# Idle products of the identity ahead of the matmul groups of a state-space kernel's front, on one Trainium2 core

## The chip, the core and the metric

The kernel runs on one core of one Trainium2 chip. The metric is the device time of one execution in microseconds (us). A profiled execution gives the trace from which all spans and durations below come; its own time and the medians of the timed runs are in the table further down.

## What is computed

The reference is one transformer-like block on a sequence of L = 2048 rows of D = 640 features, all in float32. Six modulation vectors come from a small product, `mod = silu(c) @ w_mod`. Then:

```
h = layernorm(x) * (1 + ca) + sa
x = x + ga * conv(h)            # S4: y = irfft(rfft(h) * rfft(K)) + h * Dskip
h = layernorm(x) * (1 + cb) + sb
x = x + gb * (silu(h @ w1) * (h @ w3)) @ w2     # F = 1728
```

The convolution kernel is `K[d, l] = Re sum_n C[d,n] dt B[d,n] exp(dt A[d,n] l)` with N = 128 complex states for each of the 640 features. The convolution needs tables of exp, sin and cos for all d and n, products of these, and Fourier transforms along l.

## The kernel before, in words

The 640 features are cut into 40 steps of 16 (`NS = 40`, `SD = 16`). A step's convolution kernel is made in a pipeline with these parts; the names are those of the code, and L numbers are lines of the kernel:

- `phases` (L485, GpSimd) multiplies integer phases, `absph`, `cosine`, `sine` (L493 to L503, ScalarE) turn them into cos and sin.
- `exp_fast` (L445) and `exp_slow` (L454) put the logarithms of the magnitudes into PSUM by matmuls (tiles `pa`, `pq`), and `fast` and `slow` (L464, L469, ScalarE) take their exp into a table `A`.
- `real1`, `real2`, `imag1`, `imag2` (L512 to L526, VectorE) multiply magnitudes by cos and sin.
- `kgen` (L532) contracts over n on TensorE (64 matmuls of 32 columns, tile `pk`), `k1evac` (L542, VectorE) scales the result, `k_stage1` (L551) is the first stage of the Fourier transform (tile `pt`), and `k_out` (L559, ScalarE) stores it in `uk`.

Ahead of that stand the tables' parameters (`class Polar`, L243): its `rows` (L291) transposes logarithms on TensorE into the tables `la` and `lm` (tile `pT`, L305 to L308). It runs once for the first 128 features and once for the other 512 (`rest`). The modulation vectors come from `mod_early` (L333, eight pieces), `mod_shift` (L342), `mod_gate` (L359) and, later, `mod_cols` (L368, five pieces): matmuls of `w_mod` columns (`mod_sums`, L319), a VectorE copy, and small matmuls on that copy. The input itself is normalized (`ln1_norm`, L392) and goes through the first Fourier stage in 16 tiles of 128 rows (`u_stage1`, L411): 8 small matmuls of 32 rows by 64 columns for each tile, 12 for an even tile, in two PSUM tiles `pu`, then a ScalarE or VectorE evacuation of each into `u`, and a DMA of `u` to DRAM (`us`).

The part up to where the first `stage2` (L576, tile `p`) runs is called the front here. In it the order of each engine's work is chosen by the scheduler of the framework from the order of the program. Behind the front, from L861 on, `in_order[0]` is true, and the order is a list written out by hand (`ROUND`, L854). The front begins with the first `Polar`, makes the tables of steps 0 and 1 (L758 to L767), and only then starts the tiles of `u` (`u_stage1(0)`, L780). The loop at L799 goes over ten values of `tk`; each does one step's tables, `kgen` of the step before, `k_stage1` of the one before that, and for `tk < 6` two tiles of `u`. At `tk` 2 and 6 it makes the exponentials of four steps.

Five tags of PSUM tiles share the 8 banks. `A` and `B` hold `pT`, `pa`, `pq` and the second half of `pu`, `Z` holds `pr`, the `pm` of `mod_cols` and of one piece of `mod_early`, and the first half of `pu`, `pb` and `pk` hold `pm`, `pk`, `pg` and `pt`. Each has one buffer, so a new tile waits until the last reader of the old one is done.

All loads and the `us` stores of the front are issued on SyncE's queue (SP), in order. Five late pieces of `w_mod` (L846) go to two places in turn, so the third, fourth and fifth each wait until the `mod_cols` that reads the place has run. The reload of `us` for the first chunk (`u_load`, L566) is issued at `tk` 7, between the fourth and the fifth of these pieces. `mod_cols(4)` (L801) is the last thing of the front ahead of the first `stage2`.

Far behind the front, the kernel has an idle product already: `keep_warm` (L929) multiplies a tile of zeros, 28 times in all.

Of the kernel before, what the change touches and what calls it, by code (L numbers as in the profile page):

```python
# [17 lines left out]
P = 128  # L18
# [90 lines left out]
def tile_kernel(ctx: ExitStack, tc: tile.TileContext, a):  # L109
    nc = tc.nc  # L110
    V, S, G, PE = nc.vector, nc.scalar, nc.gpsimd, nc.tensor
# [7 lines left out]
    ident = cp.tile([P, P], F32, name="ident")  # L119
# [8 lines left out]
    in_order = [False]  # L128
# [59 lines left out]
    lt = pm_.tile([P, 2, D - DC], F32, name="lt")  # L188
# [51 lines left out]
        [w_room(1, 0, 256, 1280), w_room(1, 1, 256, 1280), w_room(1, 2, 256, 1280), w_table(), w_table()])]  # L240


    class Polar:  # L243

        def __init__(self, cs, E, l2):
# [45 lines left out]
        def rows(self):  # L291

            nt = 2 * self.nk
            nat = lambda v: v.rearrange("n (t p r j) -> n t r p j", t=nt, p=4, r=2)
            rows = lambda v: v[:, :self.nk * P].rearrange("n (t r p j) -> n t r p j", t=nt, p=4, r=2)
            for k in range(nt):
                self.E.tensor_tensor(rows(lt[:, 0])[:, k], nat(self.are)[:, k], nat(self.dtc)[:, k], op=OP.mult)
            for k in range(nt):
                V.tensor_tensor(rows(lt[:, 1])[:, k], nat(self.q)[:, k], nat(self.ld)[:, k], op=OP.add)
            for i, dst in enumerate((la, lm)):  # L300
                raw = lt[:, i, :self.nk * P].rearrange("n (b c) -> n b c", c=32)
                both = self.l2[i].rearrange("n (b s c) -> n b s c", s=2, c=32)
                acopy(both.bitcast(F32R)[:, :, 0], raw)
                V.tensor_tensor(both[:, :, 1], raw, both[:, :, 0], op=OP.subtract)
                pT = psS.tile([P, 2, 512], F32, name="pT", tag="AB"[i], bufs=1).rearrange("p a b -> p (a b)")  # L305
                for k in range(nt):
                    PE.transpose(pT[:, k * P:(k + 1) * P], self.l2[i][:, k * P:(k + 1) * P], ident)
                acopy(dst[:, 2 * self.k0:2 * self.k0 + nt], pT[:, :nt * P].rearrange("p (k n) -> p k n", k=nt))  # L308
# [24 lines left out]
    def mod_early(i, w, tag):  # L333

        pm = psS.tile([P, 512], F32, name="pm", tag=tag, bufs=1)
        n = w.shape[2]
        part = mod_sums(w, pm)
        for b in range(n // P):
            PE.matmul(pm[:, 256 + b:257 + b], part[:, b * P:(b + 1) * P], one4, start=True, stop=True)
        V.tensor_copy(cols.rearrange("p s k -> p (s k)")[:, 2 * i:2 * i + n // P], pm[:, 256:256 + n // P])  # L340

    def mod_shift():  # L342

        sa, ca, ga, zero, inv, r, gs = (cols[:, i] for i in range(7))
        V.tensor_scalar(ca, ca, 1.0, None, op0=OP.add)
        V.tensor_scalar(zero, ca, 0.0, 1e-18, op0=OP.is_equal, op1=OP.mult)
        V.tensor_tensor(ca, ca, zero, op=OP.add)
        V.reciprocal(inv, ca)
        V.tensor_tensor(r, inv, sa, op=OP.mult)

        pr = psS.tile([P, 2, 512], F32, name="pr", tag="Z", bufs=1).rearrange("p a b -> p (a b)")
        for k in range(KD):
            PE.matmul(pr[:, k * P:(k + 1) * P], r[:, k:k + 1].broadcast_to([P, P]), ident, start=True, stop=True)
        for hh in range(2):
            h = slice(hh * 64, hh * 64 + 64)
            act(shift[h], pr[h, hh * 320:hh * 320 + 320], AF.Copy, scale=c1c[h])
        V.tensor_copy(rrow[:64], pr[:64, :D])

    def mod_gate():  # L359

        V.tensor_tensor(cols[:, 6], cols[:, 1], cols[:, 2], op=OP.mult)
        gt = pm_.tile([P, WC], F32, name="part", bufs=2)[:, :KD * NA].rearrange("p (k g) -> p k g", k=KD)
        V.tensor_tensor(gt, bc(tog, 1, KD), bc(cols[:, 6], 2, NA), op=OP.mult)
        pg = psS.tile([P, 512], F32, name="pg", tag="pb", bufs=1)
        PE.matmul(pg[:, :KD * NA], toq, gt.rearrange("p k g -> p (k g)"), start=True, stop=True)
        V.tensor_copy(gaT, pg[:, :KD * NA])

    def mod_cols(i, w):  # L368

        pm = psS.tile([P, 2, 512], F32, name="pm", tag="Z", bufs=1)  # L370
        part = mod_sums(w, pm[:, 0])
        lo, hi = ((0, 3), (0, 3), (0, 3), (0, 1), (2, 3))[i]
        for b in range(lo, hi):
            PE.matmul(pm[:, 1, b:b + 1], part[:, b * P:(b + 1) * P], one4, start=True, stop=True)
        V.tensor_copy(modTf[:, 3 * i + lo:3 * i + hi], pm[:, 1, lo:hi])
        if i >= 3:

            row = part[:, P:] if i == 3 else part[:, :2 * P]
            PE.matmul(pm[:, 1, 256:], one4.broadcast_to([P, P]), row, start=True, stop=True)
            V.tensor_copy(gbr[:, (i - 3) * 256:(i - 3) * 256 + 256], pm[:, 1, 256:])  # L380
        if i == 4:
            V.tensor_scalar(modT[:, 1, :], modT[:, 1, :], 1.0, None, op0=OP.add)
# [28 lines left out]
    def u_stage1(j):  # L411


        x = xt[j]
        u = hpz.tile([P, 4, D // 2], F32, name="u", bufs=2)
        pu = [psS.tile([P, 2, 512], F32, name="pu", tag=t, bufs=1) for t in ("Z", "AB"[j % 2])]
        one = j % 2 == 0
        for q in range(2 if one else 0):
            for hh in range(2):
                PE.matmul(pu[0][hh * 64:hh * 64 + 64, q, :320], c1[q * NA:q * NA + 1],  # L420
                          rrow[q * NA:q * NA + 1, hh * 320:hh * 320 + 320],
                          start=True, stop=False, tile_position=(q * NA, hh * 64))
        for h in range(2):
            for q in range(2):
                r0 = (2 * h + q) * NA
                r = slice(r0, r0 + NA)
                for hh in range(2):
                    PE.matmul(pu[h][hh * 64:hh * 64 + 64, q, :320], s1r[r], x[r, hh * 320:hh * 320 + 320],  # L428
                              start=not (one and h == 0), stop=True, tile_position=(r0, hh * 64))
        if one:  # L430
            acopy(u[:, :2, :], pu[0][:, :, :320])
        else:
            V.tensor_tensor(u[:, :2, :], pu[0][:, :, :320], bc(shift, 1, 2), op=OP.add)
        V.tensor_tensor(u[:, 2:, :], pu[1][:, :, :320], bc(shift, 1, 2), op=OP.add)
        nc.sync.dma_start(usw[:, 4 * j:4 * j + 4, :], u)
# [4 lines left out]
    def exp_rows(s):  # L440
        return s // 4, slice(s % 4 * 8, s % 4 * 8 + 8), [(rr, slice(rr * 64, rr * 64 + 64)) for rr in range(2)]

    pA, pQ = {}, {}

    def exp_fast(steps):  # L445

        for s in steps:
            pA[s] = psS.tile([P, 2, 512], F32, name="pa", tag="AB"[s % 2] if not in_order[0] else "B", bufs=1)
            t, js, rows = exp_rows(s)
            for rr, r in rows:  # L450
                keep(PE.matmul(pA[s][:, rr, :], la[r, t, :], r2[r, js, :].rearrange("p j b -> p (j b)"),  # L451
                               start=True, stop=True, tile_position=(r.start, 0)))

    def exp_slow(steps):  # L454

        for s in steps:
            pQ[s] = psS.tile([P, 2, 512], F32, name="pq", tag="AB"[s % 2] if not in_order[0] else "B", bufs=1)
            t, js, rows = exp_rows(s)
            for i, w in enumerate((la, lm)):
                for rr, r in rows:  # L460
                    keep(PE.matmul(pQ[s][:, rr, :256], w[r, t, :], bc(sel[r, js], 2, NA) if i else r1[r, js, :],  # L461
                                   start=(i == 0), stop=(i == 1), tile_position=(r.start, 0)))
# [69 lines left out]
    def kgen(s):  # L532
        E, A = EC.pop(s), AA.pop(s)
        pk = psS.tile([P, SD // 4, NB], F32, name="pk", tag="pk", bufs=1)
        for g in range(SD // 4):
            for st, x in enumerate((E, A)):
                for dq in range(4):
                    keep(PE.matmul(pk[dq * 32:dq * 32 + 32, g, :], x[:, g * 4 + dq, 1, :], x[:, g * 4 + dq, 0:3:2, :],  # L538
                                   start=(st == 0), stop=(st == 1), tile_position=(0, dq * 32)))
        PK[s] = pk  # L540
# [10 lines left out]
    def k_stage1(s):  # L551
        pt = PT[s] = psS.tile([P, 4, P], F32, name="pt", tag="pb", bufs=1)
        kk = K1.pop(s)
        for g in range(4):
            for c in range(2):
                keep(PE.matmul(pt[c * 64:c * 64 + 64, g, :], kk[:, g, :], s1[:, c, :],  # L556
                               start=True, stop=True, tile_position=(0, c * 64)))
# [318 lines left out]
    for tk in range(NS - 4, LAG + 8 * NDC + 2):  # L876
# [14 lines left out]
        i = tk - 1 - LAG - 8 * NDC + 8  # L891
# [662 lines left out]
```

## Time and profile before

| what | us |
|---|---|
| median of 3 runs | 980.74 (979.18 to 981.52) |
| the profiled execution's own time | 979.54 |
| its span, first to last instruction | 977.8 |
| mean granted TensorE clock over the span | 0.94 |
| TensorE matmuls busy | 895.3 (92%) |
| VectorE busy | 715.4 (73%) |
| ScalarE busy | 543.6 (56%) |

The front is the first 167 us of the span. In a row of the timeline the first number is the start in us, the second the duration of the group in us, then engine, line, operation, output and inputs, and in brackets how long the engine was idle before it and what ended that. A row of the windows view gives the length of the window, and for each engine the busy time and the count of records, then PEclk, the granted TensorE clock (1.00 is full speed), the busy share of the DMA engines and the GB/s that they moved. One float32 `matmul` of the program is two MATMUL records and two weight loads (the 5 products of L353 are 10 records); a transpose is one. The clock is granted for stretches whose ends lie on a grid of 3.413 us. For the first 20 us of the span the trace holds no record of the clock, and the view shows 1.00 there.

### The profile page before, as it was taken

To read this page: it belongs to the slowest core of one execution; us is meant where nothing else is said; L and a number is where in the kernel's file an instruction comes from. 1 tells how busy PE (TensorE), PEld (TensorE's weight loads), DVE (VectorE), ACT (ScalarE), POOL (GpSimd) and SP (SyncE) were. 2 spreads that over 40 slices of the span, in tenths; PEclk is the share of its full clock that TensorE was granted. 3 is DMA by queue.
4 is the path that set the end of the run, shared out by engine and by line. 5 is a ranking of instruction groups with operands and counts; after the bars stand their busy time and mean duration, and the time that the engine had idled before them with its cause. 6 is when DMAs were issued, how large, how long until landed. Compare 5 with 4: busy or idle time off the path is not lost.

```text
span 977.8 us, 20279 instructions
## 1 busy us (share of the span) xinstructions
PE 895.3 (92%) x8050; PEld 675.2 (69%) x8050; DVE 715.4 (73%) x1257; ACT 543.6 (56%) x797; POOL 278.1 (28%) x278
## 2 busy tenths in 40 slices
PE   5779986898888889799999999999999999999998
PEld 2434444566666667467888888777888888888886
DVE  5778866999999996667666666567796766654675
ACT  3737675999999984246433333355753333333332
POOL 1372233454556550204422220121242222200000
PEclk9555587999999999999999999999999999999999
DMA  8544468556656588785312212895422221113443
GB/s 251 191 142 160 175 210 189 163 143 162 162 149 169 151 223 230 244 206 208 95 55 95 67 55 66 230 273 193 142 83 70 77 67 54 55 41 95 148 151 119
DMA packets 103715, 140.73 MB, mean 144 GB/s; under 512 B 20580, under 2 KB 62820, under 8 KB 103620
## 3 DMA queue, kind: packets, MB, share of 16 engines
q1 hardware_dynamic: 99812, 129.34, 45.2%
q0 software_dynamic: 2304, 7.74, 2.4%
q10 hardware_dynamic: 1504, 2.36, 0.8%
q8 instruction: 63, 1.03, 0.4%
q14 instruction: 32, 0.26, 0.1%
HBM read 107.94 MB, written 31.46 MB: 143 GB/s over the span
## 4 chain that ended last, share of the span: by engine, by line
PE 77%; ACT 9%; DMA 5%; DVE 4%; issue 3%; POOL 2%; ACTq 0%; SPq 0%; DVEq 0%; POOLq 0%
PE ps L103 55%; PE p L587 6%; PE pz L629 3%; PE pt L556 3%; PE pk L538 2%; ACT A L136 2%; DMA zs<-zt 2%; ACT cs L136 2%; DMA uk<-in_w_mod_dram 2%; PE pa L451 1%; PE pu L428 1%; PE pq L461 1%; PE pu L420 1%; PE pm L325 1%; ACT uk L139 1%
## 5 line engine op out<-in xcount | busy, mean ns | idle before, releaser
L103 DVE TENSOR_TENSOR s<-ps,s 128x512 f32<-128x512 f32 x138 | 94.9, 687 | 80.0 <-PE ps L103 79.7
L489 POOL TENSOR_TENSOR ph<-thi,iota 128x1024 int32<-128x1024 int32 x40 | 91.2, 2279 | 149.3 <-DVE A L525 61.1
L103 DVE TENSOR_TENSOR gl<-rw,gh 128x640 fp32r<-128x640 f32 x87 | 78.1, 898 | 66.6 <-ACT gh L103 66.5
L103 ACT CAST gh<-rw 128x640 fp32r<-128x640 f32 x87 | 63.3, 727 | 104.9 <-PE ps L103 64.9
L587 PE MATMUL p<-uk,s 128*64 128x256 f32 x640 | 79.8, 390 | 16.1 <-issue 7.2
L103 PE MATMUL ps<-xA,gh 128*128 128x512 f32 x280 | 87.8, 392 | 0.4 <-ACT xA L103 0.4
L103 PE MATMUL ps<-gh,uh 128*128 128x512 f32 x224 | 87.5, 390 | 0.0
L103 PE MATMUL ps<-gl,uh 128*128 128x512 f32 x224 | 87.2, 389 | 0.0
L103 POOL TENSOR_TENSOR S<-rw 128x256 f32<-128x256 f32 x46 | 36.8, 801 | 173.9 <-DVE S0l L103 163.1
L103 PE MATMUL ps<-gh,ul 128*128 128x512 f32 x208 | 81.1, 390 | 0.0
L587 PEld LDWEIGHTS p<-uk,s 128*64 128x64 f32 x640 | 46.1, 138 | 40.1 <-issue 12.3
L514 DVE TENSOR_TENSOR E<-A,cs 128x1024 f32<-128x1024 f32 x40 | 60.9, 1523 | 2.2 <-ACT cs L136 2.2
L103 PEld LDWEIGHTS ps<-xA,gh 128*128 128x128 f32 x280 | 52.1, 188 | 13.0 <-ACT xA L103 1.0
L103 PE MATMUL ps<-xA,gl 128*128 128x512 f32 x140 | 54.6, 390 | 0.0
L490 POOL TENSOR_TENSOR ph<-ph,phi 128x512 int32<-128x512 int32 x40 | 50.8, 1269 | 6.4 <-DVE phi L316 3.6
L556 PE MATMUL pt<-s,K 128*64 128x128 f32 x640 | 50.5, 295 | 0.6 <-ACT uk L139 0.6
L103 ACT ACTIVATE s<-ps 128x512 f32<-128x512 f32 (+1 forms) x33 | 19.7, 597 | 53.1 <-PE ps L103 53.1
L521 DVE TENSOR_TENSOR A<-A,ph 128x1024 f32<-128x1024 f32 x40 | 48.7, 1218 | 0.0
L103 PEld LDWEIGHTS ps<-gl,uh 128*128 128x128 f32 x224 | 42.1, 188 | 9.0
L103 PEld LDWEIGHTS ps<-gh,uh 128*128 128x128 f32 x224 | 42.0, 188 | 8.7
L538 PE MATMUL pk<-E 128*32 128x64 f32 x1280 | 46.0, 234 | 2.0 <-DVE E L514 1.2
L629 PE MATMUL pz<-Y,i 64*128 64x128 f32 x640 | 43.9, 280 | 4.1 <-ACT zt L139 4.0
(256 smaller groups left out, 2268.4 us busy)
## 6 DMA issues: line engine op xcount, KB each, us to landing
rw<-in_w_dram SPq DMA_DIRECT2D x52, 320.0 KB
us<-u SPq DMA_DIRECT2D x16, 640.0 KB
s<-in_s_dram SPq DMA_DIRECT2D x40, 256.0 KB
i<-in_i_dram SPq DMA_DIRECT2D x40, 256.0 KB
rw<-in_wg_dram SPq DMA_DIRECT2D x31, 320.0 KB
rw<-in_wu_dram SPq DMA_DIRECT2D x28, 320.0 KB
uk<-us SPq DMA_DIRECT2D x32, 256.0 KB
zs<-zt SPq DMA_DIRECT2D x32, 256.0 KB
```

Of the source, the lines that this page charges most:

```text
L103: ins = fn(*args, **kw)
L136: return tc.keep_in_program_order(S.activation(*args, **kw))
L139: return tc.keep_in_program_order(S.copy(out, in_))
L325: PE.matmul(pm[r, :n], scb[:, g], w[:, g, :], start=True, stop=False, tile_position=(0, r.start))
L489: hold(G.tensor_tensor(p, bc(thi[:, sl], 2, NPH), bc(iota, 1, SD), op=OP.mult))
L490: keep(G.tensor_tensor(p[:, :, :NA], p[:, :, :NA], bc(phi[:, sl], 2, NA), op=OP.add))
L514: keep(V.tensor_tensor(EC[s][:, :, 1:3, :], AA[s][:, :, 1:3, :], mid(cs[s]), op=OP.mult))
L521: keep(V.tensor_tensor(A[:, :, 1:3, :], A[:, :, 1:3, :], mid(ph[s]), op=OP.mult))
L538: keep(PE.matmul(pk[dq * 32:dq * 32 + 32, g, :], x[:, g * 4 + dq, 1, :], x[:, g * 4 + dq, 0:3:2, :], start=(st == 0), stop=(st == 1), tile ...
L556: keep(PE.matmul(pt[c * 64:c * 64 + 64, g, :], kk[:, g, :], s1[:, c, :], start=True, stop=True, tile_position=(0, c * 64)))
L587: keep(PE.matmul(p2[par * 64:par * 64 + 64, pi, c, :], s2[:, pi * 2 + par, c * 64:c * 64 + 64], uk[:, 0:kn + 1:kn, f, :], start=True, stop ...
L629: ins = keep(PE.matmul(pz[:, par, (g % 2) * 2 + pi, :], i1[r, pi, c, :], Y[r, pi, c, :], start=(c == 0), stop=(c == 1), tile_position=(par ...
```

## The change

A function is added that multiplies the 128 x 128 identity by itself into the PSUM tile that a matmul group is about to fill, `n` times. The group's first matmul starts a new sum and so overwrites the result. In the hand-ordered part it does nothing.

```
+    def stay_warm(t, n, by=None):
+
+        if in_order[0]:
+            return
+        out = t if len(t.shape) == 2 else t[:, 0] if t.shape[2] >= P else t[:, :P // t.shape[2]]
+        for _ in range(n):
+            PE.matmul(out[:, :P] if len(out.shape) == 2 else out, ident, ident if by is None else by, start=True, stop=True)
```

It is called right behind the allocation of each PSUM tile of the front:

```
 Polar.rows   pT   stay_warm(pT, 8 if i == 0 and self.cs.start == 0 else 2, lt[:, 1, :P])
 mod_early    pm   stay_warm(pm, 2)
 mod_shift    pr   stay_warm(pr, 4)
 mod_gate     pg   stay_warm(pg, 2)
 mod_cols     pm   stay_warm(pm, 2)
 u_stage1     pu   stay_warm(t, 2) for each of the two tiles
 exp_fast     pa   stay_warm(pA[s], 2)
 exp_slow     pq   stay_warm(pQ[s], 1)
 kgen         pk   stay_warm(pk, 2)
 k_stage1     pt   stay_warm(pt, 2)
```

In `Polar.rows` the product is of the identity by the first 128 columns of `lt[:, 1]`, which VectorE writes at L299. The program orders the idle products ahead of the group's own matmuls. No DMA, no tile and no instruction of another engine is added, moved or removed in the program.

More of the change, by code (lines that the diff above doesn't have):

```diff
@@ L305, in rows @@
                 pT = psS.tile([P, 2, 512], F32, name="pT", tag="AB"[i], bufs=1).rearrange("p a b -> p (a b)")
+                stay_warm(pT, 8 if i == 0 and self.cs.start == 0 else 2, lt[:, 1, :P])
                 for k in range(nt):
@@ L335, in mod_early @@
         pm = psS.tile([P, 512], F32, name="pm", tag=tag, bufs=1)
+        stay_warm(pm, 2)
         n = w.shape[2]
@@ L351, in mod_shift @@
         pr = psS.tile([P, 2, 512], F32, name="pr", tag="Z", bufs=1).rearrange("p a b -> p (a b)")
+        stay_warm(pr, 4)
         for k in range(KD):
@@ L364, in mod_gate @@
         pg = psS.tile([P, 512], F32, name="pg", tag="pb", bufs=1)
+        stay_warm(pg, 2)
         PE.matmul(pg[:, :KD * NA], toq, gt.rearrange("p k g -> p (k g)"), start=True, stop=True)
@@ L370, in mod_cols @@
         pm = psS.tile([P, 2, 512], F32, name="pm", tag="Z", bufs=1)
+        stay_warm(pm, 2)
         part = mod_sums(w, pm[:, 0])
@@ L416, in u_stage1 @@
         pu = [psS.tile([P, 2, 512], F32, name="pu", tag=t, bufs=1) for t in ("Z", "AB"[j % 2])]
+        for t in pu:
+            stay_warm(t, 2)
         one = j % 2 == 0
@@ L448, in exp_fast @@
             pA[s] = psS.tile([P, 2, 512], F32, name="pa", tag="AB"[s % 2] if not in_order[0] else "B", bufs=1)
+            stay_warm(pA[s], 2)
             t, js, rows = exp_rows(s)
@@ L457, in exp_slow @@
             pQ[s] = psS.tile([P, 2, 512], F32, name="pq", tag="AB"[s % 2] if not in_order[0] else "B", bufs=1)
+            stay_warm(pQ[s], 1)
             t, js, rows = exp_rows(s)
@@ L534, in kgen @@
         pk = psS.tile([P, SD // 4, NB], F32, name="pk", tag="pk", bufs=1)
+        stay_warm(pk, 2)
         for g in range(SD // 4):
@@ L553, in k_stage1 @@
         kk = K1.pop(s)
+        stay_warm(pt, 2)
         for g in range(4):
```

## The prediction

> **What bounds the kernel now.** I read the page first: the engines' slices and the TensorE clock (PEclk, tenths of full speed), each slice 24.4 us.
>
> ```profile
> PE   5779986898888889799999999999999999999998
> PEclk9555587999999999999999999999999999999999
> ```
>
> From the eighth slice on the clock is full and TensorE nearly always busy; the half-speed stretch lies in the front. Nothing behind the front gets another instruction, so the question is how many us earlier the front ends. Windows over its parts, cut where the path changes its engine:
>
> ```profile
> 10.00:28.00 18.00, 14.24 (x108) 8.44 (x108) 8.70 (x35) 7.77 (x14) 5.86 (x4) 0.87 0.95 277
> 28.00:78.00 50.00, 37.79 (x356) 18.38 (x356) 39.34 (x73) 28.13 (x35) 24.48 (x29) 0.53 0.48 171
> 78.00:136.00 58.00, 52.05 (x562) 27.59 (x566) 49.92 (x87) 41.50 (x51) 19.92 (x17) 0.59 0.44 160
> 136.00:167.00 31.00, 22.45 (x370) 15.12 (x362) 18.39 (x29) 20.53 (x24) 10.43 (x6) 0.83 0.94 234
> ```
>
> PE, PEld, DVE, ACT and POOL stand in this order, then PEclk. From 78 to 136 us PE is busy 52.05 of 58 us at a clock of 0.59, but VectorE is busy 49.92 as well. Then the chain of waits in three of these windows (shares by line), and the longest single piece of it:
>
> ```profile
> by line: POOL ph L489 11.2%; issue 8.2%; POOL rs L402 7.1%; POOL ph L490 6.1%; DVE u L434 5.8%; POOL lt L297 5.6%; DVE st L399 5.5%; PE pu L428 5.4%; PE pu L420 5.2%; DVE E L514 4.7%; DVE u L433 4.6%; DVE rs L403 4.2%; POOL rs L401 3.6%; PO
> by line: PE pu L428 18.9%; PE pt L556 11.2%; PE pu L420 10.9%; PE pT L307 6.6%; PE pk L538 6.3%; PE pa L451 6.0%; ACT cs L136 5.8%; ACT ph L136 5.2%; PE pq L461 4.5%; issue 4.5%; ACT u L139 4.3%; ACT uk L136 3.1%; ACT x L136 2.8%; DVE u L43
> by line: DMA uk<-in_w_mod_dram 33.5%; PE pm L325 11.0%; PE pm L374 8.1%; PE pq L461 4.9%; issue 4.8%; ACT L136 4.1%; DVE E L514 4.0%; PE pm L379 3.9%; DVE A L521 3.9%; PE pk L538 3.8%; ACT cs L136 3.7%; PE pt L556 3.6%; PE pa L451 3.5%; DVE
> 152.26 10.38 DMA uk<-in_w_mod_dram
> ```
>
> The reader is to see three different stages. From 28 to 78 us the path runs over POOL and DVE, and PE's share is small (`pu`, 5.4% and 5.2%, 5.3 us). From 78 to 136 us the seven PE groups shown make 64.4%, 37.4 us. From 136 us on a third is one wait for the last piece of `w_mod`.
>
> Why is the clock low while PE is busy? Windows of 3.413 us, PE alone, then PEclk:
>
> ```profile
> 71.11:74.53 3.41, 3.41 (x66) 0.50 0.73 244
> 74.53:77.94 3.41, 1.61 (x28) 1.00 0.69 261
> 88.18:91.59 3.41, 3.41 (x52) 0.50 0.00 0
> 91.59:95.01 3.41, 3.41 (x44) 0.50 0.02 5
> 115.49:118.90 3.41, 3.41 (x28) 0.50 0.00 0
> 118.90:122.31 3.41, 2.38 (x91) 1.00 0.64 172
> ...
> 45.37 1.37 PE L428 MATMUL pu<-x,misc 32*64 32x320 f32 x16 [0.78 <-ACT u L139]
> 88.13 1.32 PE L428 MATMUL pu<-x,misc 32*64 32x320 f32 x2
> ```
>
> The full windows at 71.11 and 115.49 are followed by a clock of 1.00, the one at 88.18 by 0.50. Busy does not say how full the array is: two `pu` records of 32 x 64 alone take 1.32 us, as long as 16 that run side by side (1.37 us). I read from this that the clock goes by the work that the array does, not by PE's busy time. The rows don't prove it: they hold no measure of how full the array was. A product of the identity fills all 128 rows and columns, so I expect it to raise the clock.
>
> The Trainium skill, TensorE: Matmul & The Clock Gate, Part 1 (The HAM clock gate), says under "What's actually happening" that the gate opens after one busy window of about 3.4 us. The trace differs: 3.41 of 3.41 us busy at 88.18, and the next window still at 0.50; the measurement decides. By that rule, products added where PE is already busy would change no clock, which is the fourth case below.
>
> **The change part by part.** It adds 180 products. Counted by the calls and by the times at which their groups run now: 24 between 10 and 28 us (8 + 2 for the first `pT`, 10 for five pieces of `mod_early`, 4 for two `pa`), 56 from 28 to 78 (32 of them for eight tiles of `u`), 72 from 78 to 136 (32 for `u`, 12 for `pa` and `pq`, 10 `kgen`, 10 `pt`, 4 `pT`, 2 `mod_cols`, 2 for the next `pa`), 28 from 136 to 167.
>
> The price of one, and what a warm clock is worth:
>
> ```profile
> 29.30 2.50 PE L353 MATMUL pr<-ident,cols 128*128 128x128 f32 x10 [2.71 <-DVE cols L349]
> 425.60 2.35 PE L103 MATMUL ps<-ident,T 128*128 128x128 f32 x20
> 96.88 1.97 PE L556 MATMUL pt<-s,K 128*64 128x128 f32 x14
> 144.53 1.09 PE L556 MATMUL pt<-s,K 128*64 128x128 f32 x16
> 17.81 0.80 PE L451 MATMUL pa<-r,la 64*128 64x512 f32 x2
> 139.19 0.40 PE L451 MATMUL pa<-r,la 64*128 64x512 f32 x2
> ...
> L103 PEld LDWEIGHTS ps<-xA,gh 128*128 128x128 f32 x280 | 52.1, 188 | 13.0 <-ACT xA L103 1.0
> ```
>
> L353 is the same form, cold: 10 records for 5 products, 0.50 us each. Warm, 20 records of that size take 2.35 us (transposes, one record each), so a product of two is 0.235. Its two weight loads of 128 columns could pace it instead, at 188 ns each 0.376. I take 0.235, because the 20 warm records load new weights each time too. Existing work: `pt` goes from 0.141 to 0.068 us a record, `pa` from 0.80 to 0.40 for two; I take 0.52 of the cold time, a saving of 0.48.
>
> *78 to 136 us.* The path's 37.4 us of PE save 18.0. Of the 72 products, those on the path: 72 x 37.4 / 52.05 = 51.7, at 0.235 12.2 us. Net -5.8. Bounds: all 72 on the path (16.9 us) leaves -1.1; all hidden, VectorE is late next, idle for 58 - 49.92 = 8.1 us, so no more than -8.1.
>
> *28 to 78 us.* The 5.3 us of `pu` save 2.5. Six products stand there on the path (tiles 0 and 1, but the last pair can run while ScalarE copies): 1.4 us. Net -1.1. The other 50 lie beside this stretch:
>
> ```profile
> 48.83 1.87 POOL ph L489
> 64.99 0.71 POOL rs L402
> ```
>
> Between these rows POOL works through phases and parameters in its queue, and the norm of the next `u` tiles waits behind. PE's 37.79 us, cold, hide here; warm 19.7 plus 56 x 0.235 = 13.2 is less, so the cover stays. If the clock stayed cold, the six would cost 3.0 and save nothing: +3.0; if they hid too, -2.5.
>
> *10 to 28 us.* The one new wait is here. The first eight products read `lt`, so they can't start before L299 is done at 11.1 us, and the whole PE queue stands behind them: the transposes for `la`, the two `pa`, the pieces of `mod_early`.
>
> ```profile
> 10.00:20.00 10.00, 9.28 (x56) 4.81 (x56) 4.31 (x17) 3.53 (x9) 1.90 (x1) 1.00 1.11 340
> 20.00:30.00 10.00, 5.66 (x57) 4.33 (x57) 5.71 (x25) 6.22 (x7) 4.86 (x5) 0.67 0.82 230
> ...
> 10.73 0.36 DVE L299 TENSOR_TENSOR lt<-uk 128x64 f32<-128x64 f32 x2
> 16.71 0.16 DVE L340 COPY cols<-pm 128x2 f32<-128x2 f32 x1 [2.49 <-PE pm L339]
> 16.79 0.22 DVE L289 TENSOR_SCALAR thi<-uk 128x128 int32<-128x128 f32 x1
> 17.08 1.90 POOL L489 TENSOR_TENSOR ph<-thi,iota 128x1024 int32<-128x1024 int32 x1 [16.64 <-DMA A<-in_w_mod_dram]
> 23.70 1.06 ACT L136 ACTIVATE cs<-ph 128x1024 f32<-128x1024 int32 x1 [6.17 <-POOL ph L490]
> ```
>
> DVE already waits 2.49 us for PE ahead of L340, and the phases on POOL and ACT stand behind that. Eight cold products are 4.0 us. If they turn the clock by about 17 us, PE's work from there to 20 us (at 9.28 us in 10, 2.8) and about half of the 5.66 us behind it, which now runs at a mean clock of 0.67, save 0.48 of 5.6, or 2.7. The other 16 cost from 0 (in the 3.76 us in which PE is idle, 18 - 14.24) to 3.8 on top; I put 0.4 there. Sum +1.7, with bounds 0 (other engines late anyway) and +5.1.
>
> *136 to 167 us.* PE is warm already, so products only cost, and the queue of SP turns that into time:
>
> ```profile
> 136.48 7.61 SPq L209 DMA_DIRECT2D uk<-in_w_mod_dram  x4
> 144.27 7.89 SPq L573 DMA_DIRECT2D uk<-us  x8
> 152.26 1.83 SPq L209 DMA_DIRECT2D uk<-in_w_mod_dram  x1
> ```
>
> The fourth late piece of `w_mod` waits in the first row for `mod_cols(1)`, the eight reloads stand behind it, the last piece behind these, and the DMA engines are then full until the piece lands (10.38 us). About ten products come ahead of that `mod_cols`: 2.35 us, less 0.35 that I allow for slack in the queue. Net +2.0, bounds 0 and +2.4. The products that follow run while DMA is waited for.
>
> Elsewhere nothing changes: no DMA is added, and a product needs only `ident` and a free bank, which the group behind it needs too.
>
> Sum: -5.8 - 1.1 + 1.7 + 2.0 = -3.2. The profiled execution's 979.5 becomes 976.3; it stands 1.2 under the median of 980.74, for which I predict 977.5.
>
> **The rivals.**
>
> *The products cost more than the clock returns (slower).* With p the price of a product, the sum is 51.7p - 18.0 + 6p - 2.5 + 7p + 10p - 0.35, where 7p stands for the first stage (1.7 at 0.235). That is 74.7p - 20.9, zero at 0.28 us. If the weight loads pace the products, p is 0.376 and the sum +7.2: 987.9. For it: each is the shortest work for its two full loads, they stand right behind the freeing of a bank, on the loop of evacuation and refill, and windows left cold push p towards 0.50. Against: the 20 warm records in 2.35 us.
>
> *Same: another engine is late next.* With VectorE busy 49.92 of 58 us, and ScalarE 41.50, their order can hold the stage so that 2 us of the 5.8 are left: -2 - 1.1 + 1.7 + 2.0 = +0.6, 981.3. For it: ScalarE's five groups in the chain from 78 to 136 us make 21.2% of it, 12.3 us between the bursts of PE. Against: VectorE's 8.1 idle us have room for the 5.8.
>
> *More is hidden.* All low bounds, -8.1 - 2.5, give 970.1. It belongs to the forecast's side.
>
> *The clock does not rise,* so the change doesn't do what it says: 51.7 x 0.50 + 3.0 + 5.1 + 2.4 = +36, 1017. Against: 72 products at 0.50 us fill the whole array for 36 of the 58 us, which no window quoted above comes near.
>
> **How the numbers follow.** Forecast and what lies below it 0.45; same 0.17; products too dear 0.32; no rise 0.06. The lower end is 970. At the upper end stand the dear products, 987.9, and the bounds added up (5.1 + 2.4 - 1.1 + 3.0 = +9.4, 990); I stop at 990 and leave out the case without a rise and the dearest part of the third. A measurement of this kernel tells about 0.2%, 2 us, from no change; the forecast of -3.2 lies only a little beyond. Chances: faster 0.45, same 0.17, slower 0.38. The likeliest case alone is 970 to 978.8.
>
> **What would show it.** PEclk near 1.00 in nearly all windows from 20 to 136 us shows the rise; if it stays 0.50, the fourth case holds. Idle products at about 0.12 us a record confirm the price, 0.19 the first rival. The ScalarE row `cs<-ph`, now at 23.70, should come about 2 us later. The last `us` store should be issued some 5 us earlier, and the first `p` of L587, now behind 167 us, about 3 us earlier. If TensorE is warm and the front's end doesn't move, VectorE's idle time between 78 and 136 us says whether it was the bound. The prediction is wrong if the order that the scheduler chooses for the front changes by more than these waits, which no row here can show.

## The result

The changed kernel takes 991.55 us (median of 4 runs, 988.78 to 992.53) against 981.13 us for the kernel before (4 runs, 979.18 to 981.66). The ratio is 1.0105, with a 95% interval from 1.008 to 1.013: 10.3 us slower. Of the runs below, two executions of before_order_128 and one each of before_order_full and before_order_pu lie over 1.5% above the fastest of their kernel, and the ratios leave them out. The profiled execution of the changed kernel took 992.53 us, its span is 990.8 us, and the mean granted clock rose from 0.940 to 0.966. Lines of the changed kernel carry its own numbers: L249 is the idle product, L443 was L428, L449 was L434, L606 was L587.

### The profile page after: what moved, and what is told of

It is laid out like the page before. It is cut to its first block, busy times and chain, and to the rows that moved or that the text cites. A ratio compares the mean times of both kernels' runs of the same rounds, so it can differ in the third digit from the quotient of the medians.

```text
span 990.8 us, 20993 instructions
## 1 busy us (share of the span) xinstructions
PE 925.5 (93%) x8410; PEld 714.5 (72%) x8410; DVE 711.9 (72%) x1257; ACT 545.0 (55%) x797; POOL 275.3 (28%) x278
## 4 chain that ended last, share of the span: by engine, by line
PE 75%; ACT 9%; DVE 7%; issue 3%; POOL 2%; DMA 2%; SPq 0%; ACTq 0%; DVEq 0%; POOLq 0%
PE ps L103 55%; PE p L606 4%; ACT cs L136 2%; PE pk L556 2%; PE pz L648 2%; PE pt L575 2%; PE pu L249 2%; ACT A L136 2%; ACT ph L136 1%; DMA zs<-zt 1%; PE pu L443 1%; DVE A L538 1%; PE pa L467 1%; PE pq L478 1%; DVE E L531 1%
## 5 line engine op out<-in xcount | busy, mean ns | idle before, releaser
L606 PE MATMUL p<-uk,s 128*64 128x256 f32 x640 | 78.0, 385 | 11.6 <-ACT uk L139 4.3
L606 PEld LDWEIGHTS p<-uk,s 128*64 128x64 f32 x640 | 44.5, 136 | 34.9 <-issue 6.7
L103 ACT ACTIVATE s<-ps 128x512 f32<-128x512 f32 (+1 forms) x33 | 19.7, 598 | 52.0 <-PE ps L103 52.0
L136 ACT ACTIVATE A<-pa 128x1024 f32<-128x1024 f32 x40 | 40.9, 1028 | 10.9 <-PE pa L467 10.4
L648 PEld LDWEIGHTS pz<-Y,i 64*128 64x128 f32 x640 | 39.1, 187 | 10.3 <-ACT zt L139 4.0
```

Of the source, the lines that this page charges most:

```text
L103: ins = fn(*args, **kw)
L136: return tc.keep_in_program_order(S.activation(*args, **kw))
L606: keep(PE.matmul(p2[par * 64:par * 64 + 64, pi, c, :], s2[:, pi * 2 + par, c * 64:c * 64 + 64], uk[:, 0:kn + 1:kn, f, :], start=True, stop ...
L648: ins = keep(PE.matmul(pz[:, par, (g % 2) * 2 + pi, :], i1[r, pi, c, :], Y[r, pi, c, :], start=(c == 0), stop=(c == 1), tile_position=(par ...
```

## The profile after

The page of the changed kernel, TensorE and its clock in 40 slices:

```profile
PE   6888989888888889989999999999999999999998
PEclk9866899999999999979999999999999999999999
```

The clock's first seven digits were `9555587` before: it did rise, and TensorE is as busy in the front as it was. The same four windows as in the prediction (PE, PEld, DVE, ACT, POOL, PEclk):

```profile
10.00:28.00 18.00, 17.65 (x150) 13.43 (x150) 7.90 (x29) 6.99 (x13) 5.86 (x4) 1.00 0.96 284
28.00:78.00 50.00, 42.01 (x335) 26.82 (x334) 34.43 (x68) 21.91 (x26) 23.58 (x27) 0.69 0.34 123
78.00:136.00 58.00, 50.33 (x584) 34.91 (x568) 42.91 (x80) 38.60 (x48) 13.91 (x15) 0.79 0.47 160
136.00:167.00 31.00, 27.86 (x440) 20.75 (x442) 15.32 (x24) 20.81 (x25) 8.05 (x6) 1.00 0.69 191
```

(The 1.00 of the first row means nothing up to 16.41 us, where the trace's first record of the clock begins.) From 28 to 136 us the clock is 0.69 and 0.79 instead of 0.53 and 0.59, and PE is still busy 42.01 and 50.33 us. What the clock saved, the products have filled again. The starts that the prediction named, in the timeline of the changed kernel:

```profile
24.50 1.06 ACT L136 ACTIVATE cs<-ph 128x1024 f32<-128x1024 int32 x1 [3.48 <-POOL ph L507]
148.43 0.81 DVE L449 TENSOR_TENSOR u<-pu,shift 128x640 f32<-128x640 f32 x1
169.06 0.57 SPq L209 DMA_DIRECT2D uk<-in_w_mod_dram  x1
184.18 1.95 PE L606 MATMUL p<-uk,s 128*64 128x256 f32 x16
```

and two of them in the kernel before:

```profile
134.25 0.81 DVE L434 TENSOR_TENSOR u<-pu,shift 128x640 f32<-128x640 f32 x1
167.26 1.12 PE L587 MATMUL p<-uk,s 128*64 128x256 f32 x4
```

The first `cs<-ph` is late by 0.8 us, the last `u` by 14.2, the issue of the last piece of `w_mod` by 16.8 (152.26 before) and the first `p` by 16.9. The end of the span is late by 13.0 (990.8 against 977.8). So most of the loss is made by the time the last `u` is done, and none of it behind the front.

Two things changed at once, though. The products take time, and the scheduler, which knew of them when it set the order, set another order: the groups of `pu`, `pk` and `pq` stand in other places on TensorE, VectorE's and GpSimd's streams differ too, and the reloads on SP are split around a piece of `w_mod`. A comparison of the two traces can't tell these apart.

## The experiments

**Theory A:** the time of the products themselves, where TensorE is on the path, makes the loss; the clock pays back only a part. **Theory B, the rival:** the order that the scheduler chose around them makes it. The experiments keep one and change the other. For that, instructions are changed after the scheduler has set the order and the waits. The us behind each ratio are (ratio - 1) times the median of the kernel before beside it; added to some 982 us they compare with the expectations.

### Products cut down, order kept

```
+    resize(nc, lambda t: 4)                                      # ..._4: 4 moving columns
+    resize(nc, lambda t: (32, 4))                                # ..._tiny: 32 weight columns, 4 moving
+    resize(nc, lambda t: (32, 4) if t == "pu" else None)         # t: the tile ahead of which the product stands
```

`before_order_...` and `tiny_order_tiny` are scheduled with the small products and so stand close to the order of before; `after_order_...` and `after_..._tiny` are scheduled with whole ones.

**before_order_4**, ratio 1.0779 (1.0757 to 1.0801), +76.6 us.

> All 180 products stay, but each moves 4 columns instead of 128, and the schedule was made with them so. The order of the work on SP and ScalarE is then that of the kernel before, on VectorE and TensorE nearly so. Theory A (the products' own time on the path makes the loss): a 4-column product still loads its weights twice, so something like a third to a half of its time stays; 980 to 986 us. Theory B (the loss is the new order of the work, that the scheduler chose because the products were there): the order of before, so 980 to 982 us. If the short products hold the clock up, either theory allows a gain: down to 975 us.

**before_order_128**, 1.0184 (1.0136 to 1.0232), +18.1 us.

> The order of the run with 4 columns, frozen, and then every product widened to the 128 columns of the changed kernel. Theory A: the products cost what they cost in the changed kernel, 989 to 993 us. Theory B: the products are hidden or paid for by the clock, and the old order is kept: 977 to 983 us. The width alone is measured by the difference to the 4-column run: over 5 us by A, under 2 us by B.

**after_order_4**, 1.0605 (1.0577 to 1.0633), +59.5 us.

> Every instruction of the changed kernel in its order and with its waits, but each of the 180 products moves 4 columns instead of 128. Theory A: most of the loss goes, 980 to 986 us. Theory B: the order stays and so does the loss, 988 to 992 us.

**after_pu_4**, 1.0179 (1.0135 to 1.0222), +17.6 us.

> The changed kernel's order and waits; only the 64 products ahead of the u tiles move 4 columns, the other 116 move 128. Theory A, with the u products as its main term (26.5 us of TensorE time, right behind the release of a bank): 4 to 8 us of the loss goes, 983 to 988 us. If the loss lies with the early and late products: 989 to 992 us. Theory B: 988 to 992 us.

In before_order_128, whole products stand in nearly the old order; it was a first sign for theory A, though dearer than theory A had said. The other three are slower than either theory had it. The trace of before_order_4 says why: one window, and then, in its timeline, two `pa` records inside it and two long behind it.

```profile
78.00:136.00 58.00, 58.00 (x401) 36.30 (x401) 30.00 (x54) 27.12 (x34) 13.20 (x19) 1.00 0.30 105
```

```profile
104.81 0.79 PE L467 MATMUL pa<-r,la 64*128 64x512 f32 x2
261.51 0.50 PE L467 MATMUL pa<-r,la 64*128 64x512 f32 x2
```

TensorE is busy 58.00 of 58 us, and yet two `pa` records take 0.79 us, as they did cold (0.80 at 17.81 us before). PEclk reads 1.00 because the trace has no record ahead of the first change of the clock, which comes at 254.67 us here, and the view shows full clock until then. A product that moves 4 columns keeps TensorE busy, as the profile counts it, without raising the clock. Nor is it cheaper. Sixteen records at the low clock, first 4 columns wide in after_order_4, then 128 wide in the changed kernel:

```profile
11.71 3.55 PE L249 MATMUL pT<-lt,ident 128*128 128x4 f32 x16
```

```profile
12.16 3.62 PE L249 MATMUL pT<-lt,ident 128*128 128x128 f32 x16
```

3.55 and 3.62 us: the moving columns don't set the price. The weight columns do, as a cut to 32 of them showed (0.15 us a product below, against 0.44 here):

**after_order_tiny**, 1.0083 (1.005 to 1.0115), +8.2 us.

> The changed kernel's order and waits, and all 180 products cut to 32 weight columns and 4 moving columns, so that almost nothing of their time is left; the clock is then left to the kernel's own work, as before. The changed kernel has 47.6 us of products on its chain of waits, 126 products of 0.38 us. Theory A (the products' own time, which the clock pays back only in part): the time of the kernel before comes back, 978 to 985 us. Theory B (the order of the work that the scheduler chose around the products): the loss stays, 988 to 996 us, since now not even the clock helps.

**after_pu_tiny**, 1.0074 (1.0047 to 1.0101), +7.3 us.

> The changed kernel's order and waits; the 64 products ahead of the u tiles cut to 32 weight and 4 moving columns, the others whole. On the chain of waits of the changed kernel stand 41 of them with 16.7 us. Theory A: up to that much goes, less what the clock falls; 978 to 986 us. Theory B: 988 to 994 us. A third reading, that the u products hold the clock up for the stretch from 28 to 123 us: slower than the changed kernel, 994 us and more.

**after_early_tiny**, 1.0117 (1.008 to 1.0153), +11.5 us.

> The changed kernel's order and waits; the products ahead of the transposes, the small matmuls of the modulation and the row broadcast (14 before pT, 26 before pm, 4 before pr) cut to 32 weight and 4 moving columns, the others whole. On the chain of the changed kernel they have 10.7 us. Theory A: 2 to 8 us go, 984 to 990 us. If they are what opens the clock at 16.4 us and so pay for themselves: 990 to 996 us. Theory B: 989 to 993 us.

**after_late_tiny**, 1.007 (1.0045 to 1.0095), +6.9 us.

> The changed kernel's order and waits; the products ahead of the exponential's tables, the kernel generation and its first stage (pa, pq, pg, pk, pt: 72 in all) cut to 32 weight and 4 moving columns, the others whole. On the chain of the changed kernel they have 20.3 us. Theory A: 5 to 12 us go, 980 to 987 us. If they hold the clock up behind 122 us: 988 to 994 us. Theory B: 989 to 993 us.

**tiny_order_tiny**, 1.0155 (1.0119 to 1.0191), +15.2 us.

> The scheduler is given the 180 products at 32 weight and 4 moving columns, and they run so. This is the order of the two runs before_order_4 and before_order_128, which is that of before on SP, ScalarE and GpSimd and moves 51 of VectorE's and 130 of TensorE's instructions. Theory B, if small moves do little: 980 to 985 us. If already these moves cost: 986 us and more, and then the 1005.75 us of before_order_128 hold an order's price too.

after_order_tiny and the three runs with one group cut fell in or near theory B's ranges, and for a while that looked like its proof. It was not, because the cut products are not free:

```profile
L249 PE MATMUL pu<-ident 128*32 128x4 f32 x128 | 9.9, 190 | 16.3 <-ACT u L139 12.9 <-DVE u L448 2.1 <-DVE u L449 0.8
L249 PEld LDWEIGHTS pu<-ident 128*32 128x32 f32 x128 | 7.8, 137 | 28.2 <-ACT u L139 19.4 <-issue 3.2 <-DVE u L448 2.3
```

128 records in 9.9 us are 0.15 us a product, without any gain in the clock (0.929 over this span). One group at a time, the cut products come in the sequence in which the groups taken out come below: late 6.9, `pu` 7.3, early 11.5; the first two are not told apart in either set, as their intervals overlap. ("Early" stands for all products ahead of `pT`, `pm` and `pr`. Ten of them, ahead of the `pm` of `mod_cols`, in fact run between 148 and 180 us of the changed kernel.) Why tiny_order_tiny, nearer to the order of before, is slower still, these runs don't settle.

### Whole products in the order of before

```
+            out.append(mybir.InstMatmult(..., ins=(ident, ident), outs=(the tile's first 128 columns,),
+                sync_info=SyncInfo(on_wait=the waits of the first matmul into the tile, on_update=[])))
```

**before_order_full**, 1.0197 (1.0162 to 1.0232), +19.4 us.

> The kernel before, scheduled without any product; once its order stands, the products go into TensorE's stream ahead of the first matmul of their tile and take over its waits: 170 of the 180 (the first 8 before pT and the first 2 before pm would have to wait for the identity and are left out). Every instruction of the kernel before keeps its place. Theory B (the order that the scheduler chose makes the loss): as the changed kernel and its copy with shrunk products differ by about nothing, the products and the clock pay each other off here too, 976 to 985 us. Theory A (the products' own time): 988 to 998 us.

**before_order_no_pu**, 1.0196 (1.0157 to 1.0235), +19.3 us.

> As the run with 170 products in the order of before, but without the 64 ahead of the u tiles: 106 products. Theory B: 975 to 985 us. Theory A: 984 to 990 us. If the u products pay for themselves by the clock, this is slower than the run with 170 by 2 us or more; if they only cost, faster by 2 to 10 us.

**before_order_pu**, 1.0131 (1.0089 to 1.0173), +12.9 us.

> The order of before with the 64 products ahead of the u tiles alone. Theory B: 976 to 986 us. Theory A: 984 to 990 us.

Here nothing of the old order moved, and the loss is nearly twice that of the change. (The first 8 products ahead of `pT` and the first 2 ahead of `pm` are missing, and two `pa` records still take 0.79 us at 22.30 us, so the clock rises later than in the changed kernel.) In before_order_full:

```profile
78.00:136.00 58.00, 55.90 (x629) 35.18 (x630) 46.21 (x94) 39.41 (x49) 15.07 (x16) 0.97 0.47 171
```

```profile
by line: PE pu L443 36.8%; PE pu L435 14.7%; PE pa L467 8.8%; DVE u L448 6.0%; PE pq L478 4.2%; PE pg L377 4.2%; PE pt L575 3.6%; PE pk L556 3.3%; DVE A L538 3.0%; issue 2.8%; POOL rs L414 2.5%; PE pm L349 2.1%; DVE u L449 1.8%; POOL rs L41
```

The clock is 0.97 from 78 to 136 us, and TensorE is busy 55.90 of 58 us. The second view is the chain of waits from 68 to 108 us; the inserted products carry the line of their group there, and the TensorE pieces shown make 77.7%. At full clock TensorE has become the bound. The three losses don't add up: 64 products 12.9, the other 106 19.3, together 19.4; the two smaller sets are dearer than either theory had put them, and the runs don't show why. Nor do they show how much of the difference to the 10.3 us of the changed kernel comes from the other order and how much from the missing first products.

### The order of the changed kernel, products taken out

```
+    drop(nc, lambda t: False)                                    # none; others: t != "pu" and so on
...
+                if i.name in names and not keep(names[i.name].split("_")[0]):
...
+                    continue                                     # its waits go to the next matmul
```

**after_order_none**, 1.0018 (1.0001 to 1.0034), +1.8 us.

> The changed kernel's schedule, from which all 180 products are then taken out; the next matmul takes over their waits. So this is the order of the changed kernel without a single product. Theory A (the products' own time on TensorE, which the clock pays back only in part; the shrunk products of the runs before still cost 0.18 us each): 979 to 985 us. Theory B (the order itself costs): 988 us and more.

**after_order_no_pu**, 1.0052 (1.0034 to 1.0071), +5.1 us.

> The changed kernel's order with the 64 products ahead of the u tiles taken out, 116 left. Theory A: 981 to 988 us. Theory B: 987 to 993 us, as the changed kernel.

**after_order_no_early**, 1.0128 (1.0092 to 1.0163), +12.6 us.

> The changed kernel's order without the 44 products ahead of the transposes, the modulation's matmuls and the row broadcast, 136 left. Theory A: 984 to 990 us; if they pay for themselves by opening the clock: 990 us and more. Theory B: 988 to 993 us.

**after_order_no_late**, 1.0037 (1.0018 to 1.0056), +3.6 us.

> The changed kernel's order without the 72 products ahead of the exponential's tables, the kernel generation, its first stage and the group table, 108 left. Theory A: 980 to 987 us. Theory B: 988 to 993 us.

**after_order_early**, 1.0022 (0.9998 to 1.0045), +2.2 us.

> The changed kernel's order with only its 44 early products (14 ahead of pT, 26 ahead of pm, 4 ahead of pr); the 64 ahead of the u tiles and the 72 late ones are taken out. If the early ones pay for themselves by opening the clock, as the run without them (995.45 us) suggests: 978 to 983 us, below the 983.95 us of the order with no product. If that was an effect of the others standing at a low clock: 984 to 987 us.

This decides it. The order alone costs 1.8 us; the 180 products in it cost the other 8.5 of the 10.3 (by the ends of the two intervals, between 4.5 and 12.7). Theory B falls. Without the `pu` products 5.2 us come back, without the late ones 6.7. The early ones alone cost 0.4 us, no more than the intervals; that taking them out of the whole is slower (12.6 against 10.3) isn't told apart either, the intervals overlap.

**only_early**, 0.9982 (0.9958 to 1.0006), -1.8 us.

> The changed kernel with the calls ahead of pT and of the early pm alone (14 and 16 products, 30 in all), scheduled anew with them, so that nothing is taken out afterwards. If opening the clock early is worth its price: 977 to 981 us, faster than before. If not: 982 to 986 us.

```
-        stay_warm(pr, 4)
-        stay_warm(pg, 2)
-        stay_warm(pm, 2)                                         # mod_cols; pu, pa, pq, pk and pt too
```

The one version that these runs point to keeps the 30 products ahead of `pT` and the early `pm` and has its own schedule. It can't be told from the kernel before. Products into a bank of their own, which would not wait for a group's bank, are not among these runs: the kernel's tiles use all eight banks.

## Why the prediction was wrong

It forecast 977.5 us and named the right mechanism as its first rival, "the products cost more than the clock returns", at 987.9. The runs showed that one.

**The price of a product** failed first. The prediction took 0.235 us, from 20 transposes, and left 0.376, two weight loads, to the rival. The groups by tile in the changed kernel (busy us, mean ns of a record; two records a product):

```profile
L249 PE MATMUL pu<-ident 128*128 128x128 f32 x128 | 26.5, 354 | 11.0 <-ACT u L139 7.8 <-DVE u L448 1.2 <-DVE rrow L368 1.0
L249 PEld LDWEIGHTS pu<-ident 128*128 128x128 f32 x128 | 21.4, 243 | 21.2 <-ACT u L139 12.3 <-issue 3.6 <-DVE u L449 1.5
L249 PE MATMUL pt<-ident 128*128 128x128 f32 x32 | 6.1, 317 | 0.0
L249 PEld LDWEIGHTS pt<-ident 128*128 128x128 f32 x32 | 4.6, 207 | 0.8 <-issue 0.2
```

26.5 us for 64 products are 0.41, 6.1 for 16 are 0.38. The rival's formula, 74.7p - 20.9, is +7.5 at 0.38; the products cost 8.5. That it comes so near is partly luck: its count of products on the path was too low (below), the return that it took off was not the one that came, and 0.38 is here not the pace of two loads but a mean of cold and warm products (0.58 and 0.32 us each in a pair, below). The 20 transposes stood in one run behind one another, 0.12 a record. A product here mostly comes in a pair, then other work: four records take 0.64 us warm, 0.16 each, and 1.15 cold, by the chain of waits of the changed kernel:

```profile
101.91 0.64 PE pt L249 x4
...
106.79 0.42 PE pu L249 x2
...
142.63 1.09 PE pu L249 x8
```

A lone product, the second row, takes 0.42 us, 0.21 a record; four in a row, the third, take 1.09, 0.14 a record. So it is mostly the short run that makes the records dearer than 0.12.

The Trainium skill, TensorE: Matmul & The Clock Gate, Part 2 (LDWEIGHTS (loading the stationary operand)), says that the time of a weight load goes by the columns of the weights. The runs agree in direction: the loads ahead of `pu` take 323 ns with 128 weight columns at the low clock (before_order_4, the row below) and 137 ns with 32, mostly at the low clock (after_order_tiny, above). A quarter of the columns takes 0.42 of the time there, not a quarter.

```profile
L249 PEld LDWEIGHTS pu<-ident 128*128 128x128 f32 x119 | 27.6, 323 | 17.0 <-issue 9.3 <-ACT u L139 1.8 <-ACT cs L136 1.0
```

**How many stand on the path** failed with it. The prediction's formula had 74.7. Adding the L249 pieces of the chain of waits of the changed kernel, from 11.64 us (0.73 us, `pr`, 2 records) to 179.63 us (0.64 us, `pm`, 4 records), gives 61 pieces with 47.6 us and 126 products: 41 ahead of `pu`, 56 late ones, 29 early. By the windows of the prediction, with its numbers in brackets, these are 23 up to 28 us (7), 14 from 28 to 78 (6), 41 from 78 to 136 (51.7) and 48 behind that (10). The last is the large miss. Work has slid behind 136 us, and where the prediction let the products "run while DMA is waited for", this chain has no DMA piece behind 136 us, and TensorE's instead.

**28 to 78 us, "-1.1", and its cover.** "The other 50 lie beside this stretch" was wrong. The chain of after_order_none from 28 to 115 us, shares by line:

```profile
by line: POOL ph L506 9.1%; DMA us<-u 8.3%; DVE st L412 7.4%; issue 7.0%; DVE E L531 6.0%; POOL rs L415 5.8%; POOL ph L507 5.4%; DVE A L538 5.2%; DVE A L542 3.8%; DVE u L449 3.6%; PE pu L443 3.0%; DVE rs L416 2.8%; DVE u L448 2.6%; POOL lt 
```

and that of the changed kernel:

```profile
by line: PE pu L249 12.8%; PE pu L443 8.6%; POOL ph L506 7.5%; DVE st L412 5.0%; PE pa L249 3.9%; PE pu L435 3.8%; DVE E L531 3.5%; POOL rs L415 3.2%; POOL ph L507 3.1%; POOL lt L305 3.1%; DVE A L542 3.0%; PE pq L478 2.7%; PE pa L467 2.7%; 
```

With the same order, the chain goes over GpSimd, VectorE and DMA without the products, and over TensorE with them: its two largest shares are the products ahead of `pu` and the `pu` groups themselves. Piece by piece, behind the same end of GpSimd's work (`rs` L415 at 63.28 and 63.77 us), first without them:

```profile
69.88 1.39 PE pu L443 x14
71.29 0.82 DVE u L448
72.11 0.73 DVE u L449
72.84 0.79 DVE st L412 x2
```

and with them:

```profile
70.58 1.15 PE pu L249 x4
71.74 1.25 PE pu L443 x2
72.99 1.15 PE pu L249 x4
74.14 1.29 PE pu L443 x14
75.44 2.15 PE pu L249 x8
77.58 0.57 PE pu L435 x4
```

The prediction compared PE's total with its total before, 19.7 + 13.2 against 37.79. But the `pu` groups can't run beside GpSimd's work, they come behind it in a burst, and so do their products. And the idle time ahead of a group isn't filled: the product waits for the bank that the group waits for, and then delays it. In the timeline:

```profile
88.80 2.07 PE L249 MATMUL pu<-ident 128*128 128x128 f32 x8 [0.81 <-ACT u L139]
90.81 1.37 PE L443 MATMUL pu<-x,misc 32*64 32x320 f32 x16
```

0.81 us of idle time behind ScalarE's copy, then four products in 2.07 us, and only then the group.

**78 to 136 us, "-5.8".** Both halves were off. The clock:

```profile
84.68:88.09 3.41, 3.31 (x30) 0.50 0.67 233
88.09:91.50 3.41, 2.70 (x24) 0.50 0.58 192
91.50:94.91 3.41, 3.41 (x26) 0.50 0.57 230
94.91:98.32 3.41, 3.41 (x18) 0.50 0.77 256
98.32:101.74 3.42, 3.42 (x70) 0.50 0.00 0
101.74:105.15 3.41, 3.41 (x36) 1.00 0.00 0
```

Five windows in a row at 0.50, three of them full and with products in them; that a product "fills all 128 rows and columns, so I expect it to raise the clock" holds only in part. In such windows a pair costs 1.8 times as much (1.15 against 0.64 us), which the prediction had in a bound and in its rivals, but not in its sum. The whole account, from 7 us to the first `p`, PE busy in after_order_none:

```profile
7.00:172.24 165.24, 110.41 (x1392) 66.43 (x1392) 118.74 (x235) 99.13 (x126) 58.15 (x55) 0.73 0.60 187
```

and in the changed kernel, then its products alone:

```profile
7.00:184.18 177.18, 155.97 (x1752) 109.19 (x1753) 117.09 (x237) 100.27 (x126) 59.05 (x55) 0.85 0.56 175
7.00:184.18 177.18, 72.75 (x360) 0.85 0.56 175
```

Existing work fell from 110.41 to 155.97 - 72.75 = 83.2 us: the clock returned 27 us of TensorE's time, and the products took 73. (The 20.9 of the formula counts the path alone. On all of TensorE's time from 28 to 136 us, 37.79 + 52.05 us, the prediction's 0.48 would be 43, so the clock returned less than forecast.) That the end is late by far less than these 46 us is because the rest lay in TensorE's idle time.

**10 to 28 us, "+1.7".** `cs<-ph` is late by 0.8 us against the kernel before, where about 2 were expected. But the order alone makes it 1.9 us earlier (21.83 us in after_order_none), so the products add 2.7. By the first `u` of L449 (48.18 us in after_order_none, 51.13 in the changed kernel) they add 3.0. The term was too low by about 1 us, and inside its bounds. **136 to 167 us, "+2.0".** The first `p` is late by 16.9 us, the last `u` by 14.2, so 2.7 are added here. But after_order_none also has 2.5 of that kind:

```profile
136.73 0.81 DVE L449 TENSOR_TENSOR u<-pu,shift 128x640 f32<-128x640 f32 x1
172.24 1.08 PE L606 MATMUL p<-uk,s 128*64 128x256 f32 x8
```

2.5 us late at the last `u` (134.25 before), 5.0 at the first `p` (167.26). By these single traces it is the order that adds them, not the products, which was the caveat of the last sentence but stood in no term. Of the 11.9 us that the products add up to the first `p`, 2.7 come back later: the ends of the two spans, 990.8 and 981.6, are 9.2 apart. These runs don't show how.

**The other rivals.** VectorE was not late next: it is busy 42.91 of 58 us, and the two largest shares of the chain above are TensorE's. The clock did rise, but not to full. And the rule of the Trainium skill that the prediction weighed (TensorE: Matmul & The Clock Gate, Part 1, The HAM clock gate), that one busy window raises the clock, differs further from the trace: 58 of 58 us busy in before_order_4 at the low clock.

## What to carry to other kernels

Work that is added to raise a clock has to be priced in the short groups and partly at the low clock in which it will run, not by a long warm run, and has to be put where the engine idles: a filler that writes where the next group writes waits with it and then delays it. Before a new order is blamed, take the added work out of the new order: here the order cost 1.8 us and the work 8.5. Price an experiment's shrunken instruction too; it may not be free.

## What the runs showed of the hardware

- Busy time of TensorE, as the profile counts it, doesn't by itself raise its clock: 4-column products kept it busy for 58 of 58 us, two `pa` records took the cold 0.79 us up to 211.35 us and 0.50 from 258.43 us on, and the first record of the clock begins at 254.67 us. What share of the array's work is needed was not found; five windows with whole products in them stayed at 0.50 as well.
- PEclk shows 1.00 ahead of the first recorded change, whatever the clock is. There the durations of a known record tell it.
- A product of 128 weight columns costs the same with 4 moving columns as with 128 (3.55 and 3.62 us for 16 records, cold).
- Executions of one program vary, in part with the clock: among the twelve of only_early, those of 974.07 to 976.57 us had mean clocks of 0.945 to 0.951 and those of 982.80 to 984.92 us 0.937 to 0.942, but in after_order_none 980.73 us went with 0.944 and 987.36 us with 0.946.
